# Keys loaded in runs of four rows and turned by two DMA transposes, in a windowed attention feeding a two-layer network

## The chip, the cores and the metric

The kernel runs on one core of one Trainium2 chip. The metric is the device time of one execution in microseconds (us); for the kernel before, three runs gave 308.81, 308.98 and 309.48, median 308.98. Engines are named as in the profile: PE is TensorE (PEld its weight loads), DVE is VectorE, ACT is ScalarE, POOL is GpSimd, SP is SyncE, which here only issues DMAs. A q after a name (SPq) means the engine's instruction queue.

## The reference

Attention with a causal window of 64 positions over q, k, v of shape (batch 8, heads 8, sequence 576, head size 64), all float32, and then a two-layer network on the 4608 rows of 512 that result:

```python
scores = scale * np.matmul(q, k.transpose(0, 1, 3, 2))
rel = pos[:, None] - pos[None, :]
mask = (rel >= 0) & (rel < 64)
scores = np.where(mask, scores, -1000000000.0)
attn = np.exp(scores - np.max(scores, axis=-1, keepdims=True))
attn = attn / (np.sum(attn, axis=-1, keepdims=True) + 1e-09)
x = np.matmul(attn, v)            # heads side by side: 4608 x 512
h = x @ w_in                      # 512 x 2048
out = (h * np.cos(h)) @ w_out     # 2048 x 512
```

## The kernel before

**Tiles.** The 576 positions of a batch are nine blocks of 64 (`NU`). A block of queries sees its own 64 keys and the 64 before, so a unit `(b, p, j)` is batch b, pair of heads p (four pairs), block j, and its scores are 128 rows (two heads by 64 queries) by 128 keys (block 0: 64). Up to four units make a group that shares a PSUM bank and the steps behind it. The two heads of a pair lie in the two halves of the partitions; `qB` (`qblocks`, `qsets`) holds q with zeros in the other head's half, so that one matmul gives both heads.

**Steps of a group.** `g_scores` (matmuls `s_ps <- kT, qB`, L303), `g_max` (DVE adds the mask and takes the row's extreme, L324), `g_exp` (ACT, L336), `g_inv` (DVE), `g_norm` (`w <- e, rden`, mostly POOL, L353), `g_trans` (the weights turned by a DMA transpose from SP, `wT <- w`, L367). `values` (L384) multiplies `wT` with v into `o_ps`; `put_x` copies that to `xT`.

**Stages.** The network works on tiles of 512 rows (`mt` 0 to 8). In a stage PE computes h for one tile (64 matmuls, L453), each of 16 results going through a sine on ACT (L595) and a product on DVE (`gT`, L598), and then `out` (64 matmuls, L609). Between these matmuls the attention of the next batch is put: in the stage of tile `mt` batch `mt + 1`, whose scores fall in the second half of the stage. `values` for the next tile ends the stage, and h of that tile needs `xT`. Tile 2 takes blocks 7 and 8 of batch 1 and blocks 0 to 5 of batch 2, six groups of four units; tile 3 the rest of batch 2 and blocks 0 to 4 of batch 3.

**What sets the order.** All engines run their instructions in the order in which the program gives them. The first 57 us follow a list written by hand (`FIRST`, each word a step: `Lk2.0` loads chunk 0 of k of batch 2, `Gs` is `g_scores` and so on). Then a plan rules: `at(time, step)` gives a step a time in steps of the main loop, 32 (`T`) to a stage, 16 for h and 16 for `out`, and `pump(time)`, called after each h result and after every four matmuls of `out`, hands out all steps that are due, in order of time. So the times fix the order on every engine, SP's and POOL's queues too; nothing overtakes. `t0 = T * (b - 1)` is where the stage that holds batch b's scores begins; the scores start at `t0 + 14.6`, their `wT` from 3.8 steps later on.

**Loads and turns before.** POOL issues the loads of q, k and v, which also make them bf16. For b of 2 and up q and k come in six chunks of 96 rows each (`load_chunk`, L182), all heads side by side. k is turned by six DMA transposes per batch from SP (`turn_k`, L260), one for each chunk. q is turned by PE (`transposed`, L219, 24 of 96 columns for a whole batch) and copied to `qB` by DVE (`put_block`); in batches 4 to 6 two chunks of six, in batch 7 all six, are instead turned by DMA (`turn_q`, L244, into the one tile `turned`) and spread to `qB` by DVE (`put_turned`).

Of the kernel before, what the change touches and what calls it, by code (L numbers as in the profile page):

```python
# [10 lines left out]
def _safe_warn(msg, *a, **kw):  # L11
# [31 lines left out]
DIRECT = (0, 7, 8)  # L43
OUTS = 3
FILL = (6, 12)
TURNED = {4: 2, 5: 2, 6: 2, 7: 6}

# [24 lines left out]
)  # L72


# [1 line left out]
def kernel(  # L76
# [79 lines left out]


    def rows_tile(name):
        return ld.tile([128, NC * H * D], BF16, tag=name, name=name)

    def load_heads(name, b, p0=0, n=PAIRS):
        if (name, b) not in st:
# [15 lines left out]
    def load_chunk(name, b, c):  # L178
        if (name, b) not in st:
            st[name, b] = rows_tile(name)[0:NP].rearrange("p (c x) -> p c x", c=NC)  # L180
        src = {"q": q, "k": k}[name][b, :, c * NP:c * NP + NP]
        nc.gpsimd.dma_start(out=st[name, b][:, c].rearrange("p (h d) -> p h d", h=H),  # L182
                            in_=src.rearrange("h p d -> p h d"))

    def load_v(b, c):
        n = 128 if c < 4 else 64
# [69 lines left out]
            st.update({("kT", b, p): ka[:, p] for p in range(PAIRS)})  # L256
        return st["kA", b]

    def turn_k(b, c):
        nc.sync.dma_start(out=k_tile(b)[:, :, c * NP:c * NP + NP], in_=st["k", b][:, c], transpose=True)  # L260

    def put_k(b, p, engine="a"):
        kt = k_tile(b)[:, p]
# [18 lines left out]
    def g_scores(n, which):  # L282
        s_ps = bank((BANKS if n < n_listed else S_BANKS)[which], "s_ps")
        units = groups[n]
        if n == FILL[1]:
            nc.tensor.matmul(out=s_ps, lhsT=ident, rhs=mask16[:, 0:4].rearrange("p u c -> p (u c)"), start=True, stop=True,
                             skip_group_check=True)
        s_ps = s_ps[:, 0:len(units) * 128].rearrange("p (u c) -> p u c", c=128)
        if n < n_first:
            m0 = 2 if units[0][2] else 0  # L290
            for h in range(2):
                d = slice(64 * h, 64 * h + 64)
                nc.tensor.matmul(out=s_ps[d].rearrange("p u c -> p (u c)"), lhsT=ident[d, d],
                                 rhs=mask16[d, m0:m0 + len(units)].rearrange("p u c -> p (u c)"),
                                 start=True, stop=False, skip_group_check=True)
        for u, (b, p, j) in enumerate(units):
            kt = st["kT", b, p]
            lo, chunks = max(64 * j - 64, 0), 2 if j else 1
            rhs = kt[:, lo:lo + 64 * chunks].rearrange("d (a t) -> d a t", a=chunks)
            if j and j % 2 == 0:  # L300
                rhs = rhs[:, ::-1, :]
            if b > 1:
                nc.tensor.matmul(out=s_ps[:, u, 0:64 * chunks].rearrange("p (a t) -> p a t", a=chunks),  # L303
                                 lhsT=qblocks[(b % 2) * PAIRS + p][:, j].rearrange("d h t -> d (h t)"), rhs=rhs,
                                 start=True, stop=True, skip_group_check=True)
                continue
            for h in range(2):
                d = slice(64 * h, 64 * h + 64)
                nc.tensor.matmul(out=s_ps[d, u, 0:64 * chunks].rearrange("p (a t) -> p a t", a=chunks),  # L309
                                 lhsT=qtiles[b * PAIRS + p][d, 64 * j:64 * j + 64], rhs=rhs[d], start=n >= n_first,  # L310
                                 stop=n >= n_first or u == len(units) - 1, skip_group_check=True)
        st["s", n] = s_ps


    def g_max(n):
        s_ps, units = st["s", n], groups[n]
        negm = att.tile([128, GF], F32, tag="negm", name="negm", bufs=8)
        if n < n_first:
            nc.vector.tensor_reduce(out=negm[:, 0:len(units)], in_=s_ps, op=ALU.max, axis=AX.X, negate=True)
        else:  # L320
            s = att.tile([128, GF, 128], F32, tag="s", name="s", bufs=4)
            for u, (b, p, j) in enumerate(units):
                c = slice(0, 128 if j else 64)
                nc.vector.tensor_tensor_reduce(out=s[:, u, c], in0=s_ps[:, u, c], in1=mask[:, 2 - j % 2 if j else 0, c],  # L324
                                               scale=-scale if b else -1.0, scalar=BIG, op0=ALU.add, op1=ALU.min,
                                               accum_out=negm[:, u:u + 1])
            st["s", n] = s
        st["m", n] = negm
# [148 lines left out]
    def at(time, fn, *args):  # L477
        plan.append((time, len(plan), fn, args))
# [26 lines left out]

    for b in range(2, B):
        t0 = T * (b - 1)
        for h in range(2):
            if b in TURNED:
                at(t0 + 0.6 + 0.5 * h, put_turned, b, h, 0, 3)  # L510
            if TURNED.get(b, 0) > 2:
                at(t0 + (11 + h if TURNED[b] == NC else 10 + 0.5 * h), put_turned, b, h, 3, TURNED[b] * NP // 64)
        for c in range(TURNED.get(b, 0)):
            at(t0 - T + (24.3 if b == 4 else 23.4 if c < 2 else 26.4) + 0.01 * c, turn_q, b, c)
        for p in range(PAIRS if TURNED.get(b) != NC else 0):
            t_q = t0 + (2 if b == 2 else 1) + (3.3 if b == 2 else 3.5) * p
            for lag, fn, *args in ((0, tr_q), (0.02, put_block, 0), (0.5, put_block, 1)):
                at(t_q + lag, fn, b, p, *args)
        if b > 2:
            for c in range(NC):  # L520
                for i, name in enumerate(("q", "k")):
                    at(t0 - T + 5.6 + 1.6 * c + 0.8 * i, load_chunk, name, b, c)
        for c in range(NC):
            at(t0 + (2 + 1.2 * c if b == 2 else (-5.4, -5.3, -5.2, -4, -2.5, -1.5)[c] if TURNED.get(b) == NC else c - 5.5),
               turn_k, b, c)
        for c in range(5):
            at(t0 + (8 if TURNED.get(b) == NC else 0.5) + c, load_v, b, c)
        for half_ in range(2):
            at(t0 + ((24 if b == 3 else 22.2) + 0.1 * half_ if b > 2 else 10), spread_v, b, half_, "p" if b > 2 else "s")
    for mt in range(2, n_mt):  # L530
# [17 lines left out]
    def spread_first(lo, hi):  # L548
# [6 lines left out]
             "Lv0": lambda c: load_v(0, c), "Lv1": lambda c: load_v(1, c), "Lq2": lambda c: load_chunk("q", 2, c), "Lk2": lambda c: load_chunk("k", 2, c),  # L555
# [93 lines left out]
```

## Time and profile before

| what | value |
|---|---|
| median of three runs | 308.98 us |
| span of the profiled execution (first to last instruction) | 306.3 us |
| the profiled execution's own time | not among those shown; the median is 2.7 us above the span |
| granted TensorE clock, mean | 1.000 |
| DVE busy / ACT busy / POOL busy, share of the span | 75% / 76% / 63% |
| DMA queue of POOL's loads (q0) | 100192 packets, 18.06 MB, 80.1% of 16 engines' span |
| DMA queue of SP (q1) | 59568 packets, 23.38 MB, 40.6% |
| k loads L182 on POOL | 36, mean 783 ns |
| q transposes on PE, L219 | 96, mean 205 ns each, overlapping |
| `kT <- k` transposes from SP, issue to landing | 36, median 6.9 us |
| `wT <- w` transposes from SP, issue to landing | 68, median 4.4 us |

The busy shares are averages over stages with different limits. Durations of matmuls overlap (they are pipelined), so what a matmul costs PE is read from the chain of waits, where consecutive pieces add up. A DMA has two durations: the time in which SP or POOL is busy issuing it, during which nothing behind it in that queue is issued, and the time until its data has landed.

### The profile page before, as it was taken

How to read it: one execution, taken by the hardware profiler on the slowest of the kernel's cores; microseconds unless marked ns; L12 is line 12 of the kernel's file. 1: busy time of each engine (PE TensorE's matmuls, PEld its weight loads, DVE VectorE, ACT ScalarE, POOL GpSimd, SP SyncE). 2: the span in 40 equal slices, each digit the busy share in tenths (PEclk: the TensorE clock that was granted, in tenths of full speed). 3: DMA queues.
4: the chain of work that ended last, by engine and by line, in shares of the span. 5: the costliest groups of instructions: out<-in, count | busy, mean ns of one | idle time of the engine just before them, and what ended most of it. 6: DMA issues, size and time to landing. Idle time of an engine off the chain costs nothing.

```text
span 306.3 us, 7904 instructions
## 1 busy us (share of the span) xinstructions
PE 296.2 (97%) x2616; PEld 159.0 (52%) x2616; DVE 228.5 (75%) x908; ACT 234.3 (76%) x785; POOL 192.5 (63%) x228
## 2 busy tenths in 40 slices
PE   3889999999999999999999999999999999999996
PEld 2768844545555555445544555454545554454443
DVE  5999978599769976798579857986698668235801
ACT  5998799677997799779976997699879986116600
POOL 8998579995659669967998599959903930000000
PEclk9999999999999999999999999999999999999999
DMA  7999999999999995999999999999794643011011
GB/s 146 179 212 192 200 180 130 121 149 191 226 113 116 175 223 80 121 133 232 125 121 137 231 143 104 157 221 148 86 137 107 169 78 141 2 68 71 1 67 70
DMA packets 159945, 42.14 MB, mean 138 GB/s; under 512 B 148256, under 2 KB 155168, under 8 KB 159904
## 3 DMA queue, kind: packets, MB, share of 16 engines
q0 software_dynamic: 100192, 18.06, 80.1%
q1 hardware_dynamic: 59568, 23.38, 40.6%
q8 instruction: 20, 0.33, 0.4%
q14 instruction: 21, 0.17, 0.2%
q10 hardware_dynamic: 144, 0.20, 0.2%
HBM read 36.70 MB, written 9.44 MB: 151 GB/s over the span
## 4 chain that ended last, share of the span: by engine, by line
PE 90%; POOL 4%; DMA 2%; DVE 1%; ACT 1%; issue 1%; POOLq 0%; DVEq 0%; ACTq 0%
PE h_ps L453 35%; PE out_ps L609 35%; PE h_ps L417 5%; PE s_ps L303 4%; PE out_ps L436 4%; PE o_ps L384 3%; DMA k<-in_k_dram 2%; POOL w L353 2%; PE tq_ps L219 1%; POOL v L188 1%; PE out_ps L465 1%; PE s_ps L309 1%; PE tw_ps L364 1%; POOL w_in L204 1%; ACT e L336 1%
## 5 line engine op out<-in xcount | busy, mean ns | idle before, releaser
L609 PE MATMUL out_ps<-w_out,gT 128*128 128x512 bf16 x496 | 117.3, 379 | 0.0
L453 PE MATMUL h_ps<-xT,w_in 128*128 128x512 bf16 x512 | 115.3, 379 | 0.3
L595 ACT ACTIVATE sin<-h_ps 128x512 f32<-128x512 f32 x128 | 73.7, 598 | 32.7 <-PE h_ps L453 31.4
L598 DVE TENSOR_TENSOR gT<-h_ps,sin 128x512 bf16<-128x512 f32 x128 | 82.1, 685 | 21.9 <-ACT sin L595 21.2
L336 ACT ACTIVATE e<-s,negm 128x128 f32<-128x128 f32 (+1 forms) x256 | 97.1, 382 | 0.6 <-DVE negm L324 0.6
L353 POOL TENSOR_TENSOR w<-e,rden 128x512 bf16<-128x512 f32 (+1 forms) x74 | 70.0, 962 | 36.6 <-DVE rden L346 18.8
L453 PEld LDWEIGHTS <-w_in 128*128 128x128 bf16 x512 | 48.8, 98 | 54.7 <-issue 0.4
L609 PEld LDWEIGHTS <-gT 128*128 128x128 bf16 x496 | 45.9, 98 | 44.2
L324 DVE CUSTOM_DVE_ANT_0 s<-s_ps,mask 128x128 f32<-128x128 f32 (+1 forms) x256 | 56.4, 279 | 1.7 <-PE s_ps L309 0.9
L336 ACT ACTIVATION_READ_ACCUMULATOR e<-s,negm 128x1 f32 x256 | 48.3, 189 | 0.0
L182 POOL DMA_DIRECT2D q<-in_q_dram x36 | 28.3, 785 | 10.7 <-DMA q<-in_q_dram 4.0
L188 POOL DMA_DIRECT2D v<-in_v_dram x40 | 34.4, 878 | 0.3 <-issue 0.2
L182 POOL DMA_DIRECT2D k<-in_k_dram x36 | 28.2, 783 | 3.9 <-DMA k<-in_k_dram 1.2
L137 ACT COPY out_sb<-out_ps 128x512 f32<-128x512 f32 (+1 forms) x18 | 10.2, 566 | 24.5 <-PE out_ps L609 18.4
L346 DVE RECIPROCAL rden<-den 128x4 f32<-128x4 f32 (+1 forms) x79 | 13.1, 166 | 19.0 <-ACT e L336 18.6
L303 PEld LDWEIGHTS <-qB 128*128 128x128 bf16 x216 | 16.5, 98 | 14.2
L137 DVE CAST xT<-o_ps 128x512 bf16<-128x512 f32 x24 | 15.5, 677 | 10.1 <-PE o_ps L384 10.1
L137 DVE COPY out_sb<-out_ps 128x512 f32<-128x512 f32 x18 | 12.4, 690 | 13.2 <-PE out_ps L609 12.5
L324 DVE DVE_READ_ACCUMULATOR2_ANT negm<- 128x1 f32 x256 | 21.3, 83 | 0.0
L303 PE MATMUL s_ps<-kT,qB 128*128 128x128 bf16 (+1 forms) x216 | 21.2, 216 | 0.0
L137 POOL COPY v<-v 64x1536 bf16<-64x1536 bf16 (+3 forms) x12 | 18.8, 1570 | 0.3
L137 DVE COPY qB<-tq_ps 64x384 bf16<-64x384 bf16 (+1 forms) x40 | 15.6, 390 | 0.4
(70 smaller groups left out, 257.8 us busy)
## 6 DMA issues: line engine op xcount, KB each, us to landing
out_dram<-out_sb SPq DMA_DIRECT2D x16, 512.0 KB, 7.5
v<-in_v_dram POOLq DMA_DIRECT2D x32, 128.0 KB, 5.7
q<-in_q_dram POOLq DMA_DIRECT2D x36, 96.0 KB, 8.6
k<-in_k_dram POOLq DMA_DIRECT2D x36, 96.0 KB, 8.5
w_in<-in_moe_w_in_dram POOLq DMA_DIRECT2D x4, 512.0 KB, 8.7
w_out<-in_moe_w_out_dram POOLq DMA_DIRECT2D x4, 512.0 KB, 10.8
wT<-w SPq DMA_TRANSPOSE x68, 4.4
q<-in_q_dram POOLq DMA_DIRECT2D x7, 144.0 KB, 6.0
```

The costliest lines, as they stand in the source:

```text
L137: {"a": nc.scalar.copy, "p": nc.gpsimd.tensor_copy}.get(engine, nc.vector.tensor_copy)(out, in_)
L182: nc.gpsimd.dma_start(out=st[name, b][:, c].rearrange("p (h d) -> p h d", h=H), in_=src.rearrange("h p d -> p h d"))
L188: nc.gpsimd.dma_start(out=vt.rearrange("p (h d) -> p h d", h=H), in_=v[b, :, c * 128:c * 128 + n, :].rearrange("h p d -> p h d"))
L303: nc.tensor.matmul(out=s_ps[:, u, 0:64 * chunks].rearrange("p (a t) -> p a t", a=chunks), lhsT=qblocks[(b % 2) * PAIRS + p][:, j].rearrang ...
L324: nc.vector.tensor_tensor_reduce(out=s[:, u, c], in0=s_ps[:, u, c], in1=mask[:, 2 - j % 2 if j else 0, c], scale=-scale if b else -1.0, sc ...
L336: nc.scalar.activation(e[:, u, c], s[:, u, c], AF.Exp, bias=negm[:, u:u + 1], scale=1.0 if n < n_first else -1.0, accum_out=den[:, u:u + 1])
L353: (nc.gpsimd if engine == "p" else nc.vector).tensor_tensor(out=w[:, 0:u], in0=e[:, 0:u], op=ALU.mult, in1=rden[:, 0:u].unsqueeze(2).to_br ...
L417: nc.tensor.matmul(out=h_ps[:, half * e:half * e + half], lhsT=w_in_sb[:, ks, ff * 128:ff * 128 + 128], rhs=st["xT", 0][:, ks, half * g:ha ...
L453: nc.tensor.matmul(out=st["h", ff], lhsT=w_in_sb[:, ks, ff * 128:ff * 128 + 128], rhs=st["xT", mt][:, ks], start=start, stop=stop)
L595: nc.scalar.activation(sin, h_ps, AF.Sin, bias=math.pi / 2.0)
L598: nc.vector.tensor_tensor(out=gt[:, e], in0=h_ps, in1=sin, op=ALU.mult)
L609: nc.tensor.matmul(out=o_ps[e], lhsT=gT[ff // 2][:, ff % 2, ms * 128:ms * 128 + 128], rhs=w_out_sb[:, ff], start=ff == 0, stop=ff == n_ff - 1)
```

## The change

Four things are changed.

1. **k of batches 2 to 7.** Instead of six chunks of 96 rows, the first 512 rows come in one load in runs of four rows (`load_runs`: partition p gets rows 4p to 4p+3 of each head, 1 KB of float32 at a time) and the last 64 rows in a second (`load_rest`). DVE sorts the runs so that the row within the run comes first and the heads lie side by side (`sort_runs`, 128 x 2048 bf16). Two DMA transposes turn them: `turn_runs`, 128 x 2048, sixteen blocks of 128 columns, and `turn_rest`, 64 x 512. The buffers `rest` and `sorted` exist once.
2. **Scores.** The keys of a block now lie in four runs of 16 (32 with the block before), at a step. The matmuls of batches 2 and up read them so (`keys_of`); block 8, whose own keys are in `rest` and whose earlier ones are in the runs, takes two matmuls of 64 columns for one of 128. The scores come out in that order, and `g_max` reads PSUM at a step to put them back.
3. **q of batches 3 to 7** is turned wholly by DMA (`TURNED` 6): no PE transposes and no `put_block` there, four `put_turned` copies per batch.
4. **Times.** Sorting and turning of k go to `u0 + 14.5` (`u0 = t0 - 32`), a stage ahead of the scores, for b of 3 and up; q's loads and turns of batches 4 to 7 to `u0 + 0.6` and `u0 + 9` on; q of batch 3 is turned half at `t0 - 17` on, half at `t0`; v is loaded 5.5 steps later in batches 3 to 6, two earlier in batch 7. In `FIRST` six k loads of batch 2 become two.

```diff
-TURNED = {4: 2, 5: 2, 6: 2, 7: 6}
+TURNED = {3: 6, 4: 6, 5: 6, 6: 6, 7: 6}
+RUN = 4
...
+    def load_runs(b, lo, hi):
+        if ("raw", b) not in st:
+            st["raw", b] = rows_tile("k")[:, 0:RUN * H * D].rearrange("p (h x) -> p h x", h=H)
+        nc.gpsimd.dma_start(out=st["raw", b][:, lo:hi],
+                            in_=k[b, lo:hi, 0:128 * RUN].rearrange("h (p c) d -> p h (c d)", c=RUN))
+
+    def load_rest(b):
+        st["rest", b] = rest = ld.tile([64, H * D], BF16, tag="rest", name="rest", bufs=1)
+        nc.gpsimd.dma_start(out=rest.rearrange("p (h d) -> p h d", h=H),
+                            in_=k[b, :, 128 * RUN:S].rearrange("h p d -> p h d"))
+
+    def sort_runs(b, engine=None):
+        st["sorted", b] = to = ld.tile([128, RUN * H * D], BF16, tag="sorted", name="sorted", bufs=1)
+        copy(engine, to.rearrange("p (c h d) -> p h c d", c=RUN, h=H),
+             st.pop(("raw", b)).rearrange("p h (c d) -> p h c d", c=RUN))
...
+    def runs_of(b):
+        whole = k_tile(b).rearrange("d a s -> d (a s)")
+        return (whole[:, 0:128 * RUN * PAIRS].rearrange("d (c a p) -> d c a p", c=RUN, a=PAIRS),
+                whole[:, 128 * RUN * PAIRS:].rearrange("d (a t) -> d a t", a=PAIRS))
+
+    def turn_runs(b):
+        nc.sync.dma_start(out=runs_of(b)[0].rearrange("d c a p -> d (c a) p"), in_=st.pop(("sorted", b)), transpose=True)
+
+    def turn_rest(b):
+        nc.sync.dma_start(out=runs_of(b)[1], in_=st.pop(("rest", b)), transpose=True)
+
+    def keys_of(b, p, j):
+        runs, rest = runs_of(b)
+        n = 64 // RUN
+        if j == NU - 1:
+            return ((0, 1, rest[:, p].rearrange("d (p c) -> d c p", c=RUN).unsqueeze(2)),
+                    (1, 2, runs[:, :, p, n * j - n:n * j].unsqueeze(2)))
+        lo, chunks = max(n * j - n, 0), 2 if j else 1
+        keys = runs[:, :, p, lo:lo + n * chunks].rearrange("d c (a p) -> d c a p", a=chunks)
+        return ((0, chunks, keys[:, :, ::-1] if j and j % 2 == 0 else keys),)
...
+            if b > 1:
+                for a0, a1, keys in keys_of(b, p, j):
+                    a = 2 if j else 1
+                    nc.tensor.matmul(out=s_ps[:, u, 0:64 * a].rearrange("p (c a t) -> p c a t", a=a, c=RUN)[:, :, a0:a1],
+                                     lhsT=qblocks[(b % 2) * PAIRS + p][:, j].rearrange("d h t -> d (h t)"), rhs=keys,
+                                     start=True, stop=True, skip_group_check=True)
+                continue
...
+                to, of, add = s[:, u, c], s_ps[:, u, c], mask[:, 2 - j % 2 if j else 0, c]
+                if b > 1:
+                    to, add = (x.rearrange("q (p c) -> q p c", c=RUN) for x in (to, add))
+                    of = of.rearrange("q (c p) -> q p c", c=RUN)
...
+        u0 = t0 - T
+        if b in TURNED:
+            for c in range(NC):
+                at((t0 + (-17 + 0.8 * c if c < 3 else c - 3)) if b == 3 else u0 + 9 + 0.9 * c, turn_q, b, c)
+            for h in range(2):
+                at(t0 + 4 + 0.5 * h, put_turned, b, h, 0, 3 if b > 3 else 4)
+                at(t0 + (7.5 if b > 3 else 8) + 0.5 * h, put_turned, b, h, 3 if b > 3 else 4, NU)
...
         if b > 2:
+            at(u0 + (5.6 if b == 3 else 4.8), load_runs, b, 0, H)
+            at(u0 + (6.2 if b == 3 else 5.4), load_rest, b)
             for c in range(NC):
+                at(u0 + (6.8 if b == 3 else 0.6) + 0.7 * c, load_chunk, "q", b, c)
+        k_time = t0 + 4 if b == 2 else u0 + 14.5
+        at(k_time, sort_runs, b)
+        at(k_time + 0.1, turn_runs, b)
+        at(k_time + 0.9, turn_rest, b)
         for c in range(5):
-            at(t0 + (8 if TURNED.get(b) == NC else 0.5) + c, load_v, b, c)
+            at(t0 + (6 if b > 2 else 0.5) + c, load_v, b, c)
```

More of the change, by code (lines that the diff above doesn't have):

```diff
@@ L158, in rows_tile @@
     def rows_tile(name):
-        return ld.tile([128, NC * H * D], BF16, tag=name, name=name)
+        return ld.tile([128, NC * H * D if name == "q" else PAIRS * RC * D], BF16, tag=name, name=name)
     def load_heads(name, b, p0=0, n=PAIRS):
@@ L257, in k_tile @@
         return st["kA", b]
-    def turn_k(b, c):
-        nc.sync.dma_start(out=k_tile(b)[:, :, c * NP:c * NP + NP], in_=st["k", b][:, c], transpose=True)
+    def runs_of(b):
[15 more added lines that the diff above has]
+        return ((0, chunks, keys[:, :, ::-1] if j and j % 2 == 0 else keys),)
     def put_k(b, p, engine="a"):
@@ L301, in g_scores @@
                 rhs = rhs[:, ::-1, :]
[L302 to L306, printed above, removed]
             for h in range(2):
@@ L323, in g_max @@
                 c = slice(0, 128 if j else 64)
-                nc.vector.tensor_tensor_reduce(out=s[:, u, c], in0=s_ps[:, u, c], in1=mask[:, 2 - j % 2 if j else 0, c],
-                                               scale=-scale if b else -1.0, scalar=BIG, op0=ALU.add, op1=ALU.min,
+                to, of, add = s[:, u, c], s_ps[:, u, c], mask[:, 2 - j % 2 if j else 0, c]
+                if b > 1:
+                    to, add = (x.rearrange("q (p c) -> q p c", c=RUN) for x in (to, add))
+                    of = of.rearrange("q (c p) -> q p c", c=RUN)
+                nc.vector.tensor_tensor_reduce(out=to, in0=of, in1=add, scale=-scale if b else -1.0, scalar=BIG, op0=ALU.add, op1=ALU.min,
                                                accum_out=negm[:, u:u + 1])
@@ L507 @@
         t0 = T * (b - 1)
[L508 to L516, printed above, removed]
+        u0 = t0 - T
[5 more added lines that the diff above has]
+                at(t0 + (7.5 if b > 3 else 8) + 0.5 * h, put_turned, b, h, 3 if b > 3 else 4, NU)
+        for p in range(PAIRS if b not in TURNED else 0):
+            t_q = t0 + 2 + 3.3 * p
             for lag, fn, *args in ((0, tr_q), (0.02, put_block, 0), (0.5, put_block, 1)):
@@ L554 @@
              "Lq1": lambda p: load_heads("q", 1, p, 1), "Lk1": lambda p: load_heads("k", 1, p, 1),
-             "Lv0": lambda c: load_v(0, c), "Lv1": lambda c: load_v(1, c), "Lq2": lambda c: load_chunk("q", 2, c), "Lk2": lambda c: load_chunk("k", 2, c),
+             "Lv0": lambda c: load_v(0, c), "Lv1": lambda c: load_v(1, c), "Lq2": lambda c: load_chunk("q", 2, c), "Lk2": lambda c: load_rest(2) if c else load_runs(2, 0, H),
              "Lwi": lambda i: load_w_in(i * d_ff // W_PARTS, (i + 1) * d_ff // W_PARTS),
```

5 lines of the change are left out of this document (removed), and 6 rows, old and new, of the table FIRST.

## The prediction, made before the change was run

> **What bounds the kernel now.** I read the page's busy times first, then the chain of waits, then the timelines of the queues around the places that the change touches.
>
> ```profile
> span 306.3 us, 7904 instructions
> PE 296.2 (97%) x2616; PEld 159.0 (52%) x2616; DVE 228.5 (75%) x908; ACT 234.3 (76%) x785; POOL 192.5 (63%) x228
> ```
>
> PE has 10 us idle, nearly all before 20 us. After that only work taken from PE, or a new wait of PE, moves the end. The chain (start, us, what) shows what a stage holds:
>
> ```profile
> 88.16 1.13 PE o_ps L384 x64
> 89.32 2.75 PE h_ps L453 x12
> 92.07 0.26 PE tq_ps L219 x6
> ...
> 120.05 1.13 PE o_ps L384 x64
> ...
> 151.60 1.13 PE o_ps L384 x64
> ...
> 183.15 1.13 PE o_ps L384 x64
> ...
> 214.69 1.13 PE o_ps L384 x64
> 215.85 13.97 PE h_ps L453 x64
> ```
>
> From `o_ps` to `o_ps` batch 3's stage takes 31.9 us, those of 4 to 6 31.5 each, batch 7's (next `o_ps` 245.54) 30.85: there q has no transposes on PE, and 64 matmuls of h take 13.97. PE has no slack where it reads `wT`. SP's timeline before the `o_ps` at 88.16, SP's pace in a full stretch, and the landing of the last `wT` needed there:
>
> ```profile
> 72.19 1.33 SPq L199 DMA_DIRECT2D v<-v  x2
> 78.02 9.25 SPq L367 DMA_TRANSPOSE wT<-w  x6
> ```
>
> ```profile
> 111.96 5.46 SPq L367 DMA_TRANSPOSE wT<-w  x4
> ...
> 126.75 4.06 SPq L260 DMA_TRANSPOSE kT<-k  x3
> ```
>
> ```profile
> L367 SPq DMA_TRANSPOSE wT<-w x1: 1687/1687/1687, 85.6 to 85.6; - x1
> ...
> DMA to landing us min/median/max: 3.0/3.0/3.0
> ```
>
> SP was free from 73.6 to 78.0; the sixth `wT` lands at 88.6, and PE uses it in its last 8 of 64 matmuls, at about 89.1. SP's pitch is 4.06/3 to 5.46/4, 1.36 us a transpose. VectorE in the same stretch:
>
> ```profile
> 61.27 2.48 DVE L598 TENSOR_TENSOR gT<-h_ps,sin 128x512 bf16<-128x512 f32 x4 [1.00 <-ACT sin L595]
> ...
> 64.61 1.89 DVE L598 TENSOR_TENSOR gT<-h_ps,sin 128x512 bf16<-128x512 f32 x3
> ...
> 73.49 1.29 DVE L598 TENSOR_TENSOR gT<-h_ps,sin 128x512 bf16<-128x512 f32 x2
> 74.70 0.21 DVE L324 CUSTOM_DVE_ANT_0 s<-s_ps,mask 128x64 f32<-128x64 f32 x1
> ```
>
> After the first us it has no idle time there: whatever is put in moves all that follows. The groups kept apart by shape give the copies (busy, mean ns | idle):
>
> ```profile
> L137 DVE COPY qB<-tq_ps 64x384 bf16<-64x384 bf16 x24 | 8.4, 350 | 0.2
> ...
> L137 DVE COPY qB<-qT 64x768 bf16<-64x768 bf16 x8 | 3.0, 372 | 0.1
> ...
> L137 DVE COPY qB<-qT 64x1536 bf16<-64x1536 bf16 x2 | 1.1, 548 | 0.0
> ```
>
> And POOL's timeline has a load that waits for a turn to be done with its buffer, and the first `w` of batch 2 behind it:
>
> ```profile
> 73.53 0.77 POOL L182 DMA_DIRECT2D k<-in_k_dram  x1 [0.53 <-DMA kT<-k]
> 76.96 1.03 POOL L353 TENSOR_TENSOR w<-e,rden 128x512 bf16<-128x512 f32 x1 [2.66 <-DVE rden L346]
> ```
>
> **The change, part by part.** The sum is made on the profiled execution, span 306.3; it has no time of its own shown. The median of 308.98 is 2.7 above that span, and I add the differences to the median.
>
> *q off PE.* Batch 3 loses 24 transposes, 4 to 6 lose 16 each, 72 in all. Six take 0.26 us in the chain: 72 x 0.043 = 3.1. By stages: 31.9 - 30.85 once and about 0.7 three times, 3.15. Gain 3.15 us, and no more is to be had from PE.
>
> *PE's new work.* Block j=8 takes two matmuls of 64 columns for one of 128, 24 more in all. The group of four with one 64-column member takes 0.20 us in the chain, that of four full ones 0.22: halves cost what they hold. Bounds 0 and 24 x 55 ns = 1.3; the row nearest says 0, I take 0.3 for the further weight loads. The keys are read in runs of 16: no row has that. A gain is excluded, since 128 columns in 55 ns are the same 2.3 columns a ns as the full 512-column matmuls (x12 in 2.59 us); the bounds are 0 and a doubling of 192 x 55 + 24 x 27 ns, 11 us. I take 0 (the reversed reading of even blocks is no slower than the others in those groups).
>
> *VectorE.* Per batch 4 to 6, eight `qB` copies from PSUM of 350 ns give way to two of 1536 columns (548): -1.7 us; batch 3's eight of 576 (`qB`, 450) to four of 1024 and 1280 (about 430 and 490 on the same slope): -1.8. Added: a sort of 2048 columns, by the rows of 768 (372 ns) and 1536 (548) 0.67; by the 64x2048 copy of v 1.12. I take 0.7, whose rows have the same runs of 64. From batch 4 on this delays the first product of a group by 0.7 us and takes 1.7 from the half before: nothing: those stages have room, below. `L324` reads PSUM at a step: `qT<-tq_ps` 128x576, which reads one element in 64, takes 739 ns, some 1 ns an element like `L324` now (286 for 128, 215 for 64). Bounds 0 and 0.14 us each; at 36 a stage even 5 us lies in VectorE's idle time of the second half (106 to 123: 11.9 busy of 17). Nothing, off batch 2.
>
> *POOL and DMA.* 36 k loads of 783 ns go, six of runs (as many pieces as a v load, 0.9) and six of rest (half of one, 0.7) come: -18 us on an engine that is 63% busy, and fewer small packets. That gains nothing, since PE waits for neither. The q loads of batches 4 to 7 stand 5 steps earlier in POOL's order, ahead of nothing that is due: the next `w` comes some 14 steps later. v's loads go 5.5 steps later; they land in 5.7 us, before `spread_v` at step 22: nothing, else POOL's `w` queue behind it.
>
> *The new wait on POOL.* `load_rest(3)` overwrites the one `rest` buffer, so it waits until `turn_rest(2)` has landed; behind it in POOL stand the six q loads of batch 3, and SP's `turn_q(3, 0..2)` wait for those. `sort_runs(2)` comes after the fifth product, at 65.3, done 66.0; the two turns issue by 68.8, and land at 2.3 (the fastest `wT`) to 8.0 us (the slowest k of that stretch) after issue, the long one later; POOL is free then, so I take 70 to 72. q(3) then arrives from 76 on, in time. Beyond 75 each us would count. Batch 2's scores at 72.3 could be 2 us late at the upper bound; that costs nothing, for PE waits later anyway. The first sort also delays the products that free PE's banks by 0.7; the same holds.
>
> *SP in batch 2's stage, the term that decides.* `sort_runs(3)` stands before batch 2's first L324: 74.7 + 0.7 for the first sort + 0.7 = 76.1. Then SP issues, in this order and ahead of every `wT` of batch 2, the turn of runs(3), q 0, rest, q 1, q 2. Five at 1.37 and then five `wT` before the sixth: it starts at 76.1 + 13.7 + 0.1 = 89.9, lands 2.4 later (fastest `wT` 2.3; POOL's loads of that stretch are over by then) at 92.3, and `o_ps` ends at 92.5 instead of 89.29. Loss 3.2 to 3.3. The 0.1 is for the longer turn of 16 blocks: in SP's timeline a `wT` of three units issues in 1.20 us (at 226.78), one of four in 1.21 (at 234.05), so 12 blocks more cost 0.12 if that goes on; if the issue goes by size it is 4 x 1.2 = 4.8 us. I take the first, from two sizes measured.
>
> *Batches 3 to 7.* In each stage SP now has six q turns (8.2 us), the two k turns (2.8) and then `wT`. The q turns overwrite `turned`, so they wait for `put_turned`, which follows the ninth product: 7.8 us after the first h (2.6 + 6 x 0.86), a sine, a product and two copies of 548, 10.2 in all. For batch 3, with h from 92.6: 102.8, 111.0, 113.8, sixth `wT` issued at 120.7 and landed at 123.1; PE needs it at 92.6 + 30.7 - 1.05 + 1.0 = 123.3 (30.7 from first h to `o_ps` now). Almost no room: 0 to 1, I take 0.3. Later batches need four: landed 27.7 us after the first h, needed at about 30.5: 0.
>
> Sum: -3.15 + 3.3 + 0.3 + 0.3 = +0.7: **309.7**, own range 308.8 to 311.5.
>
> **Rivals.**
> *VectorE keeps up.* PE's last h ends at 72.45, a sine is 598 ns, a product 685: the second sort could start at 73.7 instead of 75.4 if VectorE were never behind. SP's block then starts at 74.5, 1.6 earlier: 308.1; it ends faster by over 0.2% if the block starts before 74.8. Against it: no gap at all from 61 to 76.
>
> *Long issue.* At 4.8 us the turn of runs holds SP 3.6 longer in batch 2's stage and in batch 3's, 309.7 + 7.2, about 317; the 2 us over of later batches take most of theirs. Against: 1.20 and 1.21. [...]
>
> *Strided keys.* Half rate on PE: 320. Only L303 could show it.
>
> *Clock.* PE would stand nearly idle for 3 us around 89. In this trace the same 64x512 matmul of mask (L293) takes 611 ns before 10.3 us and 383 after, so PE starts slow. If such a slow stretch, of 3 to 6 us (PE's first matmul is at 4.2), came after the wait, half of it is lost: 312. For: the start; against: some matmuls run within the wait. [...]
>
> **How the numbers follow.** Forecast 0.52, VectorE keeps up 0.15, long issue 0.12, strided 0.07, clock 0.14. Within 0.2% (308.4 to 309.6; about what a measurement can tell) lies some 0.23, nearly half of the forecast's own range; faster 0.18 (the first rival, a little of the range); slower 0.59. The range leaves out the strided and the long case, 0.19: 307.4 to 314.0, with the clock's 312 and its upper end within.
>
> **What would show it.** `tq_ps` L219 down to x24; h stages of batches 4 on near 14 us; PE idle of about 3 us before the `o_ps` near 92, ended by DMA `wT`; five SP transposes from about 76. It is wrong if `wT` starts before 81, if the turn of runs takes over 2 us to issue, or if L303 takes over 0.25 us a group of four.

## The result, and the profile after

The changed kernel takes 334.75 us (median of six, 333.35 to 339.68), the kernel before 308.89 beside it (308.4 to 309.9). The ratio is 1.082, 95% interval 1.0793 to 1.0848: 26 us slower, where 0.7 was forecast and 314 was the upper end of the range. Two of the six runs (339.36 us, the profiled one, and 339.68; mean granted clock 0.964, against 0.973 to 0.979 in the four others) were slower than the rest and are not in the ratio; the 31.3 us of the profiled span over the span before are therefore read by place, and totals are compared with the median.

The page of the changed kernel: its span, the busy times, and three rows of forty slices (PE's busy tenths, the granted clock, the DMA engines' mean busy share).

```profile
span 337.6 us, 7729 instructions
PE 301.4 (89%) x2536; PEld 159.3 (47%) x2568; DVE 227.8 (67%) x892; ACT 235.4 (70%) x785; POOL 174.3 (52%) x204
...
PE   4789999999729679999999879996999999999995
...
PEclk9999999999967959999999979997999999999999
DMA  7999999999969995399979998999999235011011
```

PE's idle time went from 10.1 us to 36.2, and its busy time from 296.2 to 301.4 although 72 transposes are gone. The holes lie at about 90 to 102 us, at 115 to 120, and near 160, 195 and 230; in or just behind most of them the granted clock is down, to 0.50 for 10.24 us from 94.6, for 6.83 from 118.5, and for 3.41 each from 197.0 and 231.1. What PE waited for from 30 to 300 us, by the waits view (total, times, longest, us):

```profile
PE o_ps L425 <- DMA wT<-w: 8.6, 6, 3.9
PE s_ps L336 <- DVE negm L366: 7.1, 3, 3.0
PE h_ps L494 <- DVE gT L641: 4.7, 1, 4.7
PE s_ps L336 <- DMA kT<-sorted: 0.5, 1, 0.5
```

The second is PE waiting for a bank of scores that `g_max` on VectorE has not yet read out, the third for a bank of h behind a late product. Only the first was in the forecast. The stages, from the first h matmul of one to the first of the next (us, from the timelines; "batch b" is the stage with b's scores):

| kernel | batch 2 | 3 | 4 | 5 | 6 | 7 |
|---|---|---|---|---|---|---|
| before | 32.15 | 31.89 | 31.55 | 31.55 | 31.54 | 30.85 |
| after | 42.63 | 40.06 | 33.26 | 35.75 | 35.57 | 30.97 |

**Batch 2's stage.** SP's timeline there, and PE's (the bracket is idle time and what ended it):

```profile
77.77 6.14 SPq L282 DMA_TRANSPOSE kT<-sorted  x1
84.00 1.72 SPq L261 DMA_TRANSPOSE qT<-q  x1
85.81 1.21 SPq L285 DMA_TRANSPOSE kT<-rest  x1
87.11 3.50 SPq L261 DMA_TRANSPOSE qT<-q  x2
90.69 10.05 SPq L408 DMA_TRANSPOSE wT<-w  x7
```

```profile
90.77 0.25 PE L425 MATMUL o_ps<-wT,v 128*64 128x64 bf16 x4
94.97 0.43 PE L425 MATMUL o_ps<-wT,v 128*64 128x64 bf16 x8 [3.95 <-DMA wT<-w]
```

The block of five turns stands where the prediction put it, but the turn of the runs alone holds SP for 6.14 us, where 1.3 was taken. The first `wT` is issued at 90.69, against 78.02 before, and the sixth at 98.23. In the same trace the same turn, of another batch, is issued in 1.67 us where none of POOL's loads is under way (at 77.77 three were):

```profile
125.80 1.67 SPq L282 DMA_TRANSPOSE kT<-sorted  x1
```

**Batch 3's stage.** VectorE's timeline: the copy of turned q stands in its queue ahead of a product, and q has not landed.

```profile
118.93 0.49 DVE L138 COPY qB<-qT 64x1280 bf16<-64x1280 bf16 x1 [6.41 <-DMA qT<-q]
119.34 0.68 DVE L641 TENSOR_TENSOR gT<-h_ps,sin 128x512 bf16<-128x512 f32 x1
```

PE, whose next bank waits for that product, is idle for 4.7 us. **Batches 4 to 6.** VectorE's waits from 140 to 260 us have three sorts that wait for runs not yet loaded; PE's 7.1 us behind `negm` lie at the same places:

```profile
DVE sorted L138 <- DMA k<-in_k_dram: 10.5, 3, 4.2
```

What the forecast had by the piece is found by the groups kept apart by shape, from 58 to 300 us (busy, mean ns | idle before):

```profile
L366 DVE CUSTOM_DVE_ANT_0 s<-s_ps,mask 128x128 f32<-128x128 f32 x196 | 45.7, 286 | 3.0 <-PE s_ps L336 2.2 <-PE s_ps L347 0.5
...
L138 DVE COPY qB<-qT 64x1536 bf16<-64x1536 bf16 x8 | 5.0, 629 | 0.1
L138 DVE COPY sorted<-k 128x2048 bf16<-128x2048 bf16 x6 | 4.1, 689 | 10.5 <-DMA k<-in_k_dram 10.5
```

So VectorE's durations were forecast nearly right, and landings were not.

### The profile page after: what moved, and what is told of

Its sections match the earlier page's. It is cut to its first block, busy times and chain, and to the rows that moved or that the text cites. A ratio compares the mean times of both kernels' runs of the same rounds, so it can differ in the third digit from the quotient of the medians.

```text
span 337.6 us, 7729 instructions
## 1 busy us (share of the span) xinstructions
PE 301.4 (89%) x2536; PEld 159.3 (47%) x2568; DVE 227.8 (67%) x892; ACT 235.4 (70%) x785; POOL 174.3 (52%) x204
## 4 chain that ended last, share of the span: by engine, by line
PE 51%; DMA 20%; POOL 11%; DVE 7%; issue 4%; ACT 4%; SPq 1%; POOLq 0%; DVEq 0%; ACTq 0%
PE out_ps L652 19%; PE h_ps L494 19%; DMA v<-in_v_dram 10%; DMA k<-in_k_dram 6%; POOL w L394 5%; PE h_ps L458 3%; PE out_ps L477 3%; DVE gT L641 3%; DMA qT<-q 3%; ACT e L377 3%; POOL q L183 2%; POOL v L138 2%; PE o_ps L425 2%; PE s_ps L336 2%; DMA wT<-w 2%
## 5 line engine op out<-in xcount | busy, mean ns | idle before, releaser
L652 PE MATMUL out_ps<-w_out,gT 128*128 128x512 bf16 x482 | 118.9, 387 | 1.0 <-issue 0.4
L494 PEld LDWEIGHTS <-w_in 128*128 128x128 bf16 x512 | 50.2, 99 | 65.8 <-issue 9.6
L652 PEld LDWEIGHTS <-gT 128*128 128x128 bf16 x496 | 46.6, 100 | 46.0 <-issue 3.2
L366 DVE CUSTOM_DVE_ANT_0 s<-s_ps,mask 128x128 f32<-128x128 f32 (+1 forms) x256 | 56.6, 278 | 3.5 <-PE s_ps L336 2.2
L336 PE MATMUL s_ps<-kT,qB 128*128 128x64 bf16 (+1 forms) x240 | 22.6, 219 | 7.6 <-DVE negm L366 7.1
L336 PEld LDWEIGHTS <-qB 128*128 128x128 bf16 x240 | 17.8, 100 | 23.9 <-DVE negm L366 8.8
L366 DVE DVE_READ_ACCUMULATOR2_ANT negm<- 128x1 f32 x256 | 21.3, 83 | 0.0
L425 PE MATMUL o_ps<-wT,v 128*64 128x64 bf16 x512 | 11.9, 202 | 8.6 <-DMA wT<-w 8.6
L138 ACT CAST xT<-o_ps 128x512 bf16<-128x512 f32 x12 | 7.0, 584 | 13.7 <-PE o_ps L425 13.1
## 6 DMA issues: line engine op xcount, KB each, us to landing
v<-in_v_dram POOLq DMA_DIRECT2D x32, 128.0 KB, 12.8
w_out<-in_moe_w_out_dram POOLq DMA_DIRECT2D x4, 512.0 KB, 10.9
```

The source lines that it names most:

```text
L138: {"a": nc.scalar.copy, "p": nc.gpsimd.tensor_copy}.get(engine, nc.vector.tensor_copy)(out, in_)
L336: nc.tensor.matmul(out=s_ps[:, u, 0:64 * a].rearrange("p (c a t) -> p c a t", a=a, c=RUN)[:, :, a0:a1], lhsT=qblocks[(b % 2) * PAIRS + p][ ...
L366: nc.vector.tensor_tensor_reduce(out=to, in0=of, in1=add, scale=-scale if b else -1.0, scalar=BIG, op0=ALU.add, op1=ALU.min, accum_out=neg ...
L425: nc.tensor.matmul(out=o_ps[64 * h:64 * h + 64, 64 * i:64 * i + 64], lhsT=vtiles[b % 2][:, max(j - 1, 0), 128 * p + 64 * h:128 * p + 64 * ...
L494: nc.tensor.matmul(out=st["h", ff], lhsT=w_in_sb[:, ks, ff * 128:ff * 128 + 128], rhs=st["xT", mt][:, ks], start=start, stop=stop)
L652: nc.tensor.matmul(out=o_ps[e], lhsT=gT[ff // 2][:, ff % 2, ms * 128:ms * 128 + 128], rhs=w_out_sb[:, ff], start=ff == 0, stop=ff == n_ff - 1)
```

## The experiments

Two theories stood at first. By the *order theory* the 26 us come from what stands ahead of what: turns ahead of batch 2's `wT` on SP, copies and sorts on VectorE whose data is not there. By the *load theory* the 18 further q turns are too much for the DMA engines wherever they stand. Times in the edits are steps of the plan (32 to a stage; `t0` begins batch b's stage, `u0 = t0 - 32`).

**k alone.** q and v as before the change.

```diff
-TURNED = {3: 6, 4: 6, 5: 6, 6: 6, 7: 6}
+TURNED = {4: 2, 5: 2, 6: 2, 7: 6}
...
-at(u0 + (6.8 if b == 3 else 0.6) + 0.7 * c, load_chunk, "q", b, c)
+at(u0 + 5.6 + 1.6 * c, load_chunk, "q", b, c)
```

> k in runs alone: q turned, loaded and copied as before, v's loads at their old times. Order theory (the loss sits in what stands ahead of what: SP's turns ahead of batch 2's wT, and copies and sorts on VectorE that wait for late landings): of the five turns ahead of batch 2's wT two are left, with an issue of some 6 us for the long one, so batch 2's stage loses 3 to 4 us, and nothing is gained on PE, since q's transposes stay; the sorts of later batches find their runs landed, for the runs now stand ahead of q in POOL's queue. 312 to 316. Load theory (the engines of the DMAs have too much to do, because of the 18 further q turns): k alone lightens them, 309 or less.

321.38 us, ratio 1.0407 (1.0339 to 1.0474): neither. Without one further q turn 12 us are lost, 7.2 of them in batch 2's stage (39.32), where PE now waits 4.1 us for k itself (`s_ps <- DMA kT<-sorted`).

**q alone.** k in chunks and v as before the change; q of 3 to 7 loaded and turned as in the changed kernel.

```diff
-TURNED = {4: 2, 5: 2, 6: 2, 7: 6}
+TURNED = {3: 6, 4: 6, 5: 6, 6: 6, 7: 6}
...
+at((t0 + (-17 + 0.8 * c if c < 3 else c - 3)) if b == 3 else u0 + 9 + 0.9 * c, turn_q, b, c)
```

> q of batches 3 to 7 turned by DMA alone, with q's new times; k in six chunks and six turns at their old times, v's loads at their old times. Order theory: three turns of 1.4 us stand ahead of batch 2's wT where SP had 4.4 us free, so batch 2's stage loses 0 to 2 us, batch 3's VectorE copies may still wait for chunks 3 to 5, and PE is relieved of 3.1 us: 307 to 313. Load theory: this is the part that costs, 325 or more.

332.21 us, 1.0758 (1.0636 to 1.0879), as the load theory has it, but not for its reason: more than half stands in one place, batch 3's stage (47.4 us), where VectorE waits 15.0 us for one turn of q. The stages of batches 4 to 6 are at 33.3 to 34.1.

**k later.** The changed kernel with k of batches 3 to 7 sorted and turned as late as its chunks were before.

```diff
-k_time = t0 + 4 if b == 2 else u0 + 14.5
+k_time = t0 + 4 if b == 2 else t0 - 5.5
```

> The changed kernel with sorting and turning of k of batches 3 to 7 put back to 5.5 steps before the stage of its scores, behind most of the wT of the batch before. Order theory: the turns of runs and rest leave the block ahead of batch 2's wT (about 7 us of 12.9), and the sorts no longer wait for runs in front of a group's first product (stages of batches 5 and 6, 4 us each): 316 to 324, with batch 3's wait for q unchanged. Load theory: nothing moves much, 330 to 336.

337.47 us, 1.0928 (1.0896 to 1.096), above both ranges and a miss for the order theory as it stood. The sorts no longer wait, but the one `rest` buffer now makes POOL wait for each late turn (3.5 to 6.7 us), v's loads come behind that, and VectorE waits 11.7 us for q of batch 3.

**q of batch 3 on PE.** The changed kernel with `TURNED` beginning at 4.

```diff
-TURNED = {3: 6, 4: 6, 5: 6, 6: 6, 7: 6}
+TURNED = {4: 6, 5: 6, 6: 6, 7: 6}
```

> The changed kernel with q of batch 3 left on PE (24 transposes and eight copies, as before), its six DMA turns gone. Order theory: batch 3's stage loses its wait for q (6.4 us of VectorE, 8.2 us of the stage) and pays 1 us for the transposes, and the block ahead of batch 2's wT shrinks by three turns, some 5 us: 320 to 325. Load theory: six turns of thirty less, a gain of 3 to 5 us: 329 to 332.

328.54 us, 1.0639 (1.0608 to 1.067): between the two. VectorE's wait in batch 3's stage is gone, yet the stage stays at 36.54: the other turns are late there too, and PE waits 2.7 us for `wT`.

**A second buffer for the last rows.** It takes away POOL's wait of 10.9 us in batch 2's stage, the "new wait on POOL" of the prediction.

```diff
-rest = ld.tile([64, H * D], BF16, tag="rest", name="rest", bufs=1)
+rest = ld.tile([64, H * D], BF16, tag="rest", name="rest", bufs=2)
```

> The changed kernel with a second buffer for the last 64 rows of k, so that POOL's load of them for batch 3 no longer waits for the turn of batch 2's (10.9 us at 75.7 in the changed kernel). If that wait is harmless, as predicted: 333 to 336 us and no stage shorter by over 1 us. If it is a cause, because q of batch 3 is loaded behind it and turned late: batch 3's stage (40.1 us) loses most of VectorE's wait of 6.4 us, 327 to 331.

338.3 us, 1.0912 (1.0852 to 1.0972): no gain, and something not expected. In the changed kernel k of batch 2 landed just in time for PE's first scores; with POOL's wait gone, batch 3's loads of q run beside its turn too, and PE waits 5.1 us. That PE waits only 0.5 us in the changed kernel was in part luck: in three other runs that keep POOL's wait, PE waits there 1.6 us (q of batch 3 on PE), 4.0 (k later) and 4.1 (k alone), for batch 3's runs are loaded ahead of the wait, beside the turn. PE's timeline, first after, then with two buffers:

```profile
74.82 0.37 PE L336 MATMUL s_ps<-kT,qB 128*128 128x64 bf16 x4 [0.51 <-DMA kT<-sorted]
```

```profile
78.05 0.55 PE L336 MATMUL s_ps<-kT,qB 128*128 128x64 bf16 x4 [5.13 <-DMA kT<-sorted]
```

**Filler for the clock.** 29 more matmuls where PE only waits in batch 2's `o_ps`.

```diff
+for _ in range({1: 20, 3: 9}.get(i, 0) if (mt, p) == (2, 0) else 0):
+    nc.tensor.matmul(out=o_ps[:, 64 * i:], lhsT=ident, start=True, stop=True, skip_group_check=True,
+                     rhs=mask16[:, 0:4].rearrange("p u c -> p (u c)")[:, 64 * i:])
```

> The changed kernel with 29 more matmuls on TensorE ahead of the second and the fourth column block of batch 2's first o_ps (20 of 128x448, 9 of 128x320, overwritten afterwards, some 5 us), where it only waits for wT. If the clock is a cause of its own: no stretch at half clock near 94.6, batch 2's stage and the start of batch 3's some 3 us shorter together, 331 to 332. If the waits alone count: 334 to 336, and what the extra matmuls don't hide is added.

340.44 us, 1.0981 (1.0792 to 1.1171). The half-clock stretch of 10.24 us from 94.6 shrinks to 3.41 us from 101.9, and no time is gained: batch 2's and 3's stages take 84.3 us together, against 82.7 in the profile after. What the slow clock costs there is not settled by it. The part of the stretch that lies in h is as long as before (3.4 us now, 3.3 then), and this run has a wait of 2.2 us at the first scores where the other has 0.5.

**SP cleared ahead of batch 2's `wT`.** q of batch 3 on PE, two `rest` buffers, and k of batch 3 turned late, so that nothing of batch 3 stands there.

```diff
+TURNED = {4: 6, 5: 6, 6: 6, 7: 6}
...
+rest = ld.tile([64, H * D], BF16, tag="rest", name="rest", bufs=2)
...
+k_time = t0 + 4 if b == 2 else t0 - 5.5 if b == 3 else u0 + 14.5
```

> The changed kernel with q of batch 3 turned by TensorE, k of batch 3 sorted and turned 9 slots later (at t0-5.5) and two buffers for the last 64 rows, so that no turn for batch 3 stands on SP's queue ahead of batch 2's wT. If the SP block of batch 2's stage is what costs there: that stage at 32 to 34 us against 42.6, and 318 to 322 in all. If the late landing of batch 2's own k and the load of the DMA engines cost it: the stage stays at 37 to 39 us, 324 to 328 in all.

334.12 us (331.24 and 337.0; too far apart for an interval, and the profile is of the longer one). `wT` is no longer late in batch 2's stage, and still the stage takes 40.36: PE waits 5.5 us for batch 2's own k. So in that stage two causes take each other's place.

**k of all batches late.** The same with every later k at `t0 - 5.5`.

```diff
-k_time = t0 + 4 if b == 2 else t0 - 5.5 if b == 3 else u0 + 14.5
+k_time = t0 + 4 if b == 2 else t0 - 5.5
```

> As the one before (q of batch 3 on TensorE, two buffers for the last rows), with k of batches 3 to 7 sorted and turned at t0-5.5, so that no sort should wait for a load that has just been issued. If the waits of the sorts (2.3 to 4.2 us in batches 4 to 6) cost what stages 5 and 6 lose: those stages at 31.6 to 32.5 us against 35.7, 311 to 315 in all. If it is the load of the DMA engines: they stay over 34, 320 to 326.

327.28 us, 1.0557 (1.0466 to 1.0648), above both ranges. No sort waits for its load any more, batch 3's stage is back at 32.01, batch 4's at 33.01; batch 2's is at 41.93, and in 4 to 6 PE waits 3.8 us for POOL's copies of v (`o_ps <- POOL v`), whose loads land 15 us after issue.

**v's loads at their old times.** All else as in the run before.

```diff
-at(t0 + (6 if b > 2 else 0.5) + c, load_v, b, c)
+at(t0 + (8 if b == 7 else 0.5) + c, load_v, b, c)
```

> The run before (k of batches 3 to 7 turned at t0-5.5, q of batch 3 on TensorE, two buffers for the last rows) with v loaded at the times of the kernel before. If the later loads of v cost nothing, as predicted: 326 to 328. If VectorE's and POOL's copies of v are what PE waits for in batches 4 to 6 there (1.6, 2.2 us and wT behind them): stages 4 to 6 at 31.6 to 32.2 us against 33.0, 35.1, 33.2, 320 to 322.

321.94 us, 1.0427 (1.0364 to 1.0491). The waits for v are gone; stages 4 and 6 are at 32.0 and 32.27, batch 5's is still at 34.3, with `wT` late by 2.7 us.

**Batch 3's loads later in the plan.**

```diff
-at(u0 + (5.6 if b == 3 else 4.8), load_runs, b, 0, H)
+at(u0 + (10 if b == 3 else 4.8), load_runs, b, 0, H)
...
```

> As the one before, with the loads of k and q of batch 3 also 4.4 slots later, behind the turn of batch 2's k on the clock (that turn takes 5 to 6 us to issue and lands 12 to 13 us after it is begun, with 7 to 8 loads of POOL's under way). If the loads under way hold up the turn: batch 2's stage loses the wait of 5 to 6.5 us at its first scores and the half clock behind it, 33 to 35 us against 41.9, 312 to 315 in all. If the size of the turn is what holds it up: the stage stays at 39 to 42 and the time at that of the run before.

321.89 us, 1.0425 (1.0403 to 1.0448), and no test at all: the loads were issued at 62.0 to 69.6, no later than before, because all that holds POOL's queue there is a wait of 1.7 us and one of 1.3, for other loads. So the later place in the plan delayed nothing, for nothing else ahead of these loads in POOL's queue held them.

**q of 4 to 7 by DMA in the kernel before.** k in chunks, no other part of the change. In this kernel the number in `TURNED` also picks times: batches 4 to 6 get those of batch 7 for v's loads too (7.5 steps later) and for k's turns (five of six 0.8 to 1.7 steps earlier).

```diff
-TURNED = {4: 2, 5: 2, 6: 2, 7: 6}
+TURNED = {4: 6, 5: 6, 6: 6, 7: 6}
```

> The kernel before with all six chunks of q of batches 4 to 7 turned by DMA (before: two of them in batches 4 to 6), at the times that batch 7's had, k in chunks as before. If a turn of q is cheap where it is late enough and nothing waits behind it: 2.4 us of TensorE's work go in three stages, 305.5 to 308.5. If the DMA engines have no room for 12 further turns: some stages with waits for qT or wT, 309 to 314.

319.35 us, 1.0349 (1.0282 to 1.0416), more than either case gave. It is the loss of the 12 further turns and of these moved times together; no run parts them. Six waits for k make up 6.4 us, with the clock halved behind two of them (0.989 on the mean):

```profile
PE s_ps L303 <- DMA kT<-k: 6.4, 6, 1.6
```

**POOL held while batch 2's k is turned.** One `rest` buffer again, and batch 3's load of it ahead of the others: what was a side effect is now used as a gate.

```diff
-at(u0 + (6.2 if b == 3 else 5.4), load_rest, b)
+at(u0 + (5.5 if b == 3 else 5.4), load_rest, b)
```

> The kernel with v back (k of 3 to 7 turned at t0-5.5, q of 3 by TensorE, v at its old times) with one buffer for the last rows again, and batch 3's load of them put ahead of its runs and its q: POOL then waits there for the turn of batch 2's last rows, and no load for batch 3 is under way while batch 2's k is turned. If the loads under way are what makes that turn late (12 to 13 us from its start to its landing; 4.3 to 4.5 in the same kernels where no load was under way): 4.5 to 7 us, PE's wait of 5.8 to 6.5 us at batch 2's first scores falls to under 1, its stage to 33 to 35 us from 41.3, and the time to 313 to 316. If the turn's own size or the sort ahead of it makes it late: over 10 us again, the stage 39 to 41, 320 to 322.

315.0 us, 1.0192 (1.0134 to 1.0249), as the loads under way have it. From its start to its landing the turn takes 6.4 us, against 13.0. First the kernel with v back, then this one: SP's line, PE's at the first scores and in `out` behind them, and the row of the DMA engines' busy share over 66 to 82 and 66 to 75 us.

```profile
68.01 6.03 SPq L282 DMA_TRANSPOSE kT<-sorted  x1
```

```profile
81.03 0.55 PE L336 MATMUL s_ps<-kT,qB 128*128 128x64 bf16 x4 [6.51 <-DMA kT<-sorted]
...
82.23 2.34 PE L652 MATMUL out_ps<-w_out,gT 128*128 128x512 bf16 x5 [0.22 <-issue]
```

```profile
DMA  9999999999999999999999999999999999999999
```

```profile
66.77 4.31 SPq L282 DMA_TRANSPOSE kT<-sorted  x1
```

```profile
73.19 0.37 PE L336 MATMUL s_ps<-kT,qB 128*128 128x64 bf16 x4
73.40 1.89 PE L652 MATMUL out_ps<-w_out,gT 128*128 128x512 bf16 x8
```

```profile
DMA  9999999999903111899941999999665005999999
```

With the loads held back the DMA engines have a hole while the runs are turned, PE's wait of 6.5 us is gone, and the stage takes 34.68 us against 41.31. It is not one lucky trace: in the three kernels with this gate PE waits at most 0.2 us there, in the five with two `rest` buffers 5.1 to 6.5. The `out` lines show the clock, granted at 0.76 over 74 to 82 us and at 0.81 over 82 to 90 in the kernel with v back: five matmuls in 2.34 us behind the wait, eight in 1.89 without it.

**k alone, held.** The same with q turned and copied as before the change; its loads keep the changed times.

```diff
-TURNED = {4: 6, 5: 6, 6: 6, 7: 6}
+TURNED = {4: 2, 5: 2, 6: 2, 7: 6}
```

> As the one before, with q of batches 4 to 7 handled as in the kernel before the change (two chunks by DMA in 4 to 6, all in 7, at the old times). What is left of the change is k in runs, sorted late. If q's further turns are what stages 4 and 5 still lose there (34.3 and 32.3 us, with waits for wT): all stages from the third on at 31.5 to 32, 311 to 313. If k in runs costs it: those stages stay over 33 together, 314 to 316.

312.58 us, 1.0101 (1.0056 to 1.0145), with all stages but batch 2's (32.77) at 32.03 or less. Its page has the clock at full speed throughout (1.000 on the mean) and PE 0.8 us busier than before: that is what k in runs costs PE.

```profile
span 308.6 us, 7874 instructions
...
PE 297.0 (96%) x2640; PEld 159.1 (52%) x2640; DVE 232.8 (75%) x914; ACT 234.8 (76%) x785; POOL 175.9 (57%) x204
...
PEclk9999999999999999999999999999999999999999
```

**q late, held.** As the one before the last, with the same q turns, but at the times that batch 7's had before the change: right ahead of the same batch's turn of k, where before they stood 13 to 17 steps ahead of it.

```diff
-at(u0 + 9 + 0.9 * c, turn_q, b, c)
+at(t0 - T + (24.3 if b == 4 else 23.4 if c < 2 else 26.4) + 0.01 * c, turn_q, b, c)
...
-at(t0 + 4 + 0.5 * h, put_turned, b, h, 0, 3 if b > 3 else 4)
+at(t0 + 0.6 + 0.5 * h, put_turned, b, h, 0, 3)
```

> As the one before the last, with all six chunks of q of batches 4 to 7 turned by DMA, at the times batch 7's had before the change (some 23 to 26 slots into the stage ahead). If 12 more turns have room there once k takes two turns and not six: stages 4 to 6 at 29.5 to 31 us, 308 to 312. If they are late again (with k in six turns they cost 1.5 us waits for kT and the clock behind them): 314 to 318.

329.41 us, 1.0658 (1.0586 to 1.073): 14 us more than with the same turns at other places, and far more than expected. SP's timeline here, then that of the 315.0 us kernel at the same place, and PE's wait here:

```profile
122.71 6.92 SPq L261 DMA_TRANSPOSE qT<-q  x5
129.72 1.31 SPq L408 DMA_TRANSPOSE wT<-w  x1
131.13 5.07 SPq L282 DMA_TRANSPOSE kT<-sorted  x1
```

```profile
124.77 2.30 SPq L282 DMA_TRANSPOSE kT<-sorted  x1
...
134.01 3.25 SPq L261 DMA_TRANSPOSE qT<-q  x2
```

```profile
PE s_ps L336 <- DMA kT<-sorted: 13.9, 4, 6.3
```

The q turns push k's into POOL's next loads: it takes 12.3 us to land, against 4.5, and PE waits 2.7 to 6.3 us for k in three stages. This settles order against load: the same turns in the same number leave the kernel 6 us or 20 behind the one before, by where they stand, and the load decides through what a turn meets under way.

None of these versions beats the kernel before. Transposes of q taken off PE are worth 3.15 us at most, some 2.1 of them in batches 4 to 6, and the mildest placing tried for those (315.0, two runs, against 312.6 without the further turns) gives that back and 2.4 us more.

## Why the prediction was wrong

The step that failed is what a DMA costs beside others. The sum took the turn of runs to be issued as fast as a small one, took landings from quick rows (2.3 us for a turn, 5.7 for v), and did not ask about those that the sorts and copies on VectorE need. So it had 3.3 us for batch 2's stage and 0.3 for the later ones; measured were 10.5, and 18.1 in batches 3 to 6. By its own terms:

*q off PE* and *PE's new work* hold. `tq_ps` is down to 24 in the changed kernel, and h of batches 4 to 7 takes 14.0 us, as forecast; k in runs adds 0.8 us to PE (0.3 taken, 0 to 1.3 bounded), and full groups of strided keys take 219 ns a matmul in the kernel with k alone held, as before, so *strided keys* falls. In the changed kernel PE's busy time is 301.4 = 296.2 - 3.15 + 0.8 + 7.5, and the 7.5 that are left are put down to the clock, 0.964 on the mean against 1.000 before (an estimate, and 32 of PE's 2568 matmuls are missing from that trace).

*VectorE*: the sort takes 689 ns (0.7), `L366` 286 as before, the turned copies of 1536 columns 629 (548 was the row). What fails is "nothing: those stages have room". It asked how long the sorts and copies run, and not whether their data is there: three sorts wait 10.5 us for their loads and the third of the four copies of batch 3's q 6.4 us for its turn, and the engine's products and extremes stand behind them. These are most of what batches 3 to 6 lose. Moving the sorts later removed those waits.

*POOL and DMA*: the "nothing" for v's later loads fails as well. With k late, PE waits 3.8 us for v; with v's old times that wait and some 5 us of the median go (327.28 to 321.94, with intervals that overlap a little). A landing of 5.7 us was assumed; the median is 12.8 in the changed kernel, and 15 are seen with k late.

*The new wait on POOL* costs nothing that shows, as forecast, and does more: it keeps batch 3's loads of q away from batch 2's turn, though not its runs. The upper bound named there ("2 us late" for the scores) is passed in all five kernels without that wait (5.1 to 6.5 us) and in two that have it (4.0 and 4.1).

*SP in batch 2's stage* has the right place, order and wait, and the wrong size. The block begins at 77.77 (76.1, in a trace that is 1.7 us late by then); the sixth `wT` is issued at 98.23 (89.9) and lands at 101.13 (92.3). Of these 8.8 us, 1.7 are the offset, 4.8 the issue of the turn of runs, and 2.3 the other issues and the landing. So the term that was to decide lost 10.5 us with what came behind it, not 3.3.

*Long issue* is the rival that comes nearest: it gave the turn 4.8 us of issue, where 6.14 were measured. But its reason, the size, is not what sets it. Both readings, 1.3 and 4.8, were made from two sizes of `wT` (1.20 and 1.21 us). One and the same turn takes 1.67 to 6.77 us in the changed kernel and up to 7.16 in the other runs, so a cost by the size alone doesn't describe it; both readings left out what is under way.

*Batches 3 to 7*, 0.3 in the sum, are the largest failure: 8.2 us in batch 3's stage and 9.9 in 4 to 6, with what was gained on PE already taken off. The step took landings 2.3 us after issue, the fastest row, in stages where the DMA engines are busy nearly all the time (90% or more in most slices of the page). In the trace the last chunk of batch 3's q lands 9.9 us after its issue has begun.

*Clock* came true behind waits, and not only at 92: in the changed kernel the granted clock is 0.50 for 23.9 us in four stretches before 235 us, 3.41, 6.83 and 10.24 us long, all multiples of 3.41. The 3 to 6 us and the half in the rival's 312 were the author's estimate from the start of the trace before, where one matmul takes 611 ns and later 383; how long PE must wait for the clock to fall no run shows. Waits of 2.13 us (the kernel with two buffers) and 2.71 (the one with v back) were followed by half clock too. The rival's 312 had one such wait, and here there were four.

What stays open: why the kernel with k alone held is still 1% slower than the one before. Its profiled span is 2.4 us longer than before, spread over batch 2's and batch 7's stage (0.6 each) and small pieces, and its times scatter from 310.1 to 314.2. No run takes that apart.

## What to carry to other kernels

Forecast a moved DMA by its landing under the load of its new place, not by the fastest row of its kind (the turn of runs landed in 4.30 to 14.97 us), and then ask what stands in line behind the instruction that needs it: a sort of 0.7 us cost 3 us of PE because it waited in VectorE's queue. One big transfer in place of six is waited for as a whole (6.5 us of PE in the kernel with v back) and held its issuing queue longer while others' loads were under way (5.86 us on the median beside five to eight of them, 2.07 beside none), so where the first consumer needs only a part, six may be better (argued from these runs, not tried by itself); a buffer that makes the loading engine wait can be a cheap gate to keep such a turn clear (6.4 us from start to landing with it, 13.0 without). Move one part at a time: here no part could be priced without what its neighbours had under way.

## What the runs showed of the hardware

The time that the same DMA transpose held SP's queue went with what was under way. The turn of 128 x 2048 was made 78 times in the changed kernel and twelve of the experiments. Counted by POOL's loads issued and not yet landed when SP began it (us, lowest, median and highest):

| POOL's loads under way | turns | issue | from start of issue to landing |
|---|---|---|---|
| none | 20 | 1.67, 2.07, 2.90 | 4.30, 4.47, 6.69 |
| 1 to 4 | 27 | 2.44, 4.25, 7.16 | 5.06, 8.09, 14.97 |
| 5 to 8 | 31 | 2.95, 5.86, 7.05 | 4.90, 10.52, 13.40 |

The four shortest issues of the last row (2.95 to 3.46, all in the kernel with k alone) had none of SP's own earlier DMAs still to land, and every other turn of that row had some, so those may count too. Why the queue is held longer beside loads, no run here shows.

The granted clock fell to 0.50 in or just behind many of PE's waits of 2 to 13 us, for 3.41 us or a multiple of it up to 13.65. The length of the wait alone doesn't decide: 2.13 and 2.71 us were followed by half clock, 2.66 (q late, held) and 2.93 (filler) were not. Matmuls within the wait don't always prevent it: in batch 2's `o_ps`, with matmuls between pieces of waiting, it stayed down for 10.24 us. Reading PSUM at a step on VectorE (286 ns for 128 x 128, as before) and keys in runs of 16 on PE (219 ns in the kernel with k alone held, as before) cost nothing that shows.
